# One-token attention plus a gated MLP on one core: w_out cut into five rows a lane and 24 lanes of ten, batches spaced by eight in the output's weights, two output stores of eight lanes

## The chip, the core and the metric

The kernel runs on 1 core of a Trainium2 chip. The metric is the device time of one execution in microseconds; a version's time is the median of its runs. Five engines work side by side, each on its own list in order: TensorE (PE, with its weight loads shown as PEld), VectorE (DVE), ScalarE (ACT), GpSimd (POOL) and SyncE (SP), which here only issues DMAs. Sixteen DMA engines move data between HBM and the on-chip memory of 128 partitions ("lanes").

## The reference

Two branches of a decode step share one normalised input, and their sum is added to the input (all bfloat16):

```python
x  = A_x                                    # (4, 1, 640)
xn = layernorm(x)
# A: attention, 32 heads of 128, one query a batch, cache of 4096 keys
q = (xn @ wq).reshape(4, 1, 32, 128)
p = softmax(q . k_cache * 128 ** -0.5)      # k_cache, v_cache: (4, 32, 4096, 128)
A = (p . v_cache).reshape(4, 1, 4096) @ wo  # wo: (4096, 640)
# B: gated MLP, Fh = 864
z = gelu(xn @ w_in)                         # w_in: (640, 1728)
g = w_sp * layernorm(z[..., 864:]) + b_sp   # one position: scalars
B = (z[..., :864] * g) @ w_out              # w_out: (864, 640)
out = x + A + B
```

The two caches are 134 MB each; wq is 5.2 MB, wo 5.2 MB, w_in 2.2 MB and w_out 1.1 MB.

## The kernel before

**Tiles and buffers.** The caches are read once, in 16 tiles each (8 heads of one batch: 8.39 MB, 65,536 bytes a lane). K tiles use two buffers (`kp`), which also hold wq at the start and the last V tile at the end. V tiles use a single buffer (`vp`), which holds the weights of branch B at the start (`w_sb`: w_in, then w_out) and wo at the end. So the first V tile can be loaded only when branch B is done with `w_sb`, and the third K tile only when the first has been used up. In the text K0, K1, ... and V0, V1, ... are these tiles.

**Start.** x is normalised and turned (`xnT_r`), wq gives the queries (`q_ps`, `qT`). All loads but three small ones go out on SP's queue, in the order in which SP's instructions stand. For this part the order is the scheduler's own: an instruction that must wait for something stands where the scheduler finds it due, and whatever follows on SP waits too.

**Branch B** (`gmlp`): 70 matmuls give z, turned, in `zT` (features on lanes); DVE and ACT apply gelu, layer norm and the gate; the result is `yT`, 128 features on lanes for each of `NFF` = 6 columns and a rest of 96. w_out's first 768 rows lie six to a lane, matching `yT`; the remaining 96 rows lie on `TL` = 16 lanes, `TK` = 6 rows each, loaded with four small DMAs of `TE` = 4 lanes. `ye_ps`/`yE` bring the rest of `yT` onto those 16 lanes with six small matmuls.

**Output.** `out_ps` is one accumulator for x, B and A: the 640 columns are cut into `NQ` = 4 parts of 160, and part q stands on lanes 32q to 32q+3, one lane a batch. `add_out` issues the four matmuls, each with a weight of four columns (the batches). At the end ACT copies `out_ps` to `res`, and four stores of four lanes each write it.

**The loop** has its order written out by hand (`tc.manual_schedule` for PE, DVE, ACT and SP). Before it stand `stage_q(0)`, `gmlp()` and V0's load. For each K tile i: `product` multiplies half the tile by the query on DVE (8.7 us), `fold` adds its halves, `sums` adds up eight-element groups on PE into `s_ps`, `row_sums` finishes the scores. One tile later follow the maximum, `exps`, `own_heads` and `weighted` (p . V on PE); after it the next V load is issued, and after `sums(i, 1)` the next K load. `group_rows`, `group_turn` and `group_proj` normalise eight heads' results, turn them (`oT`) and multiply by wo into `out_ps`. The lines that matter:

```python
stage_q(0)
gmlp()
load_v(0, v_slot("v_nat"))
for i in range(NT):
    product(i, 0)
    ...
    sums(i, 1)
    if i + 2 < NT:
        load_k(i + 2)
```

Of the kernel before, what the change touches and what calls it, by code (L numbers as in the profile page):

```python
# [10 lines left out]
BF16 = mybir.dt.bfloat16  # L11
# [6 lines left out]
def kernel(  # L18
# [45 lines left out]
    WJ = WH * Dh // P  # L64
    WW = 2
    WR = NG * ROWS
    NFF = Fh // P
    TL = 16
    TK = (Fh - NFF * P) // TL
    TE = 4  # L70
    NFC = NFF + TK
    F0 = NFF * P
    TF = TL * TK
    NZ = NFF + 1
    assert F0 + TF == Fh and TF <= P
    NQ = 4
    NO = D // NQ
    REP = GW // Bsz
# [18 lines left out]
    def v_slot(name):  # L97
# [8 lines left out]
    w_sb = v_slot("w_sb")  # L106
    w_in_sb = w_sb[:, 0 : DC * F].rearrange("p (c n) -> p c n", c=DC)
    w_out_sb = w_sb[:, DC * F : DC * F + NFC * D].rearrange("p (k n) -> p k n", k=NFC)
    nc.sync.dma_start(
        out=w_out_sb[:, 0:NFF, :], in_=B_w_out[0 : NFF * P].rearrange("(p k) n -> p k n", k=NFF)  # L110
    )
# [10 lines left out]
    for l in range(TL // TE):  # L122
        nc.sync.dma_start(
            out=w_out_sb[:TL, NFF:NFC, :].rearrange("(e l) k n -> e l (k n)", e=TE)[:, l],
            in_=B_w_out[F0:Fh].rearrange("(e l k) n -> e l (k n)", e=TE, k=TK)[:, l],
        )

    def kv_view(cache, i):
# [23 lines left out]
    WO_CUTS = ((0, WJ), (0, 11, 15, WJ))  # L152

    def load_wo():
        t = v_slot("wo")[:, 0 : HP * WJ * D].rearrange("p (g j n) -> p g j n", g=HP, n=D)
        wo_t.append(t)
        for g in range(HP):
            for j0, j1 in zip(WO_CUTS[g], WO_CUTS[g][1:]):
                nc.sync.dma_start(out=t[:, g, j0:j1, :], in_=wo_v[g][:, j0:j1, :])  # L159
# [3 lines left out]

    ident = const.tile([P, P], BF16)
    make_identity(nc, ident[:])
    ident_f = const.tile([P, P], FP32)
    nc.gpsimd.tensor_copy(out=ident_f[:], in_=ident[:])
    eps_tile = const.tile([P, 1], FP32)
# [52 lines left out]
                stop=stop,  # L221
            )

    add_out(ident[:Bsz, :GW], x_bf, start=True)


    own = const.tile([P, HT], FP32)
# [81 lines left out]
    def gmlp():  # L309
        zz, gw, gt, gz, sq = (gm[n] for n in ("zz", "gw", "gt", "gz", "sq"))  # L310
        zT = ps_pv.tile([P, 2, NZ, Bsz], FP32, tag="pv", name="zT")
        for t in range(2):
            f1 = t * Fh + F0
            w_t = w_in_sb[:, :, t * Fh : f1].rearrange("p c (f k) -> p c k f", k=NFF)
            for k in range(NZ):
                for c in range(DC):
                    nc.tensor.matmul(
                        out=zT[: P if k < NFF else TF, t, k, :],
                        lhsT=w_t[:, c, k, :] if k < NFF else w_in_sb[:, c, f1 : f1 + TF],
                        rhs=xnT[:, c, :],  # L320
                        start=(c == 0),
                        stop=(c == DC - 1),
                    )
        nc.vector.tensor_copy(out=zz[:, :, 0:NFF, :], in_=zT[:, :, 0:NFF, :])
        nc.vector.tensor_copy(out=zz[:TF, :, NFF:NZ, :], in_=zT[:TF, :, NFF:NZ, :])
        nc.vector.tensor_tensor(out=gw, in0=zz, in1=zz, op=ALU.mult)
        nc.vector.tensor_scalar(
            out=gw, in0=gw, scalar1=0.044715, scalar2=1.0, op0=ALU.mult, op1=ALU.add
# [72 lines left out]
            in1=ac_sb[:, None, Bsz : 2 * Bsz].to_broadcast([P, NZ, Bsz]),  # L401
            op=ALU.add,
        )
        yT = work.tile([P, NZ, Bsz], BF16, name="yT")
        nc.vector.tensor_tensor(out=yT[:], in0=gz[:, 0, :, :], in1=sq, op=ALU.mult)
        ye_ps = ps_m.tile([TL, TK, Bsz], FP32, tag="m", name="ye_ps")
        for k in range(TK):
            nc.tensor.matmul(
                out=ye_ps[:, k, :],
                lhsT=ident[:TF, :TF].rearrange("p (f k) -> p k f", k=TK)[:, k, :],  # L410
                rhs=yT[:TF, NFF, :],
                start=True,
                stop=True,
            )
        yE = work.tile([TL, TK, Bsz], BF16, name="yE")
        nc.scalar.copy(out=yE[:], in_=ye_ps[:])
        for k in range(NFC):
            if k < NFF:
                add_out(yT[:, k], w_out_sb[:, k, :])
            else:  # L420
                add_out(yE[:, k - NFF], w_out_sb[:TL, k, :])


    qbcs, scores, sums_ps, maxes, pms, pvs, es = {}, {}, {}, {}, {}, {}, {}
# [213 lines left out]
    def group_turn(g):  # L638
        parts = oTs[g]
        JW = WJ // WW  # L640
        t_ps = ps_m.tile([P, WJ, Bsz], FP32, tag="m", name="t_ps")
        for j in range(WJ):
            nc.tensor.matmul(
                out=t_ps[:, j, :],
                lhsT=parts[j // JW][:, j % JW, :, :],
                rhs=row_batch[:],
                start=True,
                stop=True,
            )
        oTs[g] = const.tile([P, WJ, Bsz], BF16, name=f"oT{g}")  # L650
        nc.scalar.copy(out=oTs[g][:], in_=t_ps[:])

    def group_proj(hg):
        for j in range(WJ):
            add_out(
                oTs[hg][:, j, :],
                wo_t[0][:, hg, j, :],
                stop=(hg == HP - 1 and j == WJ - 1),
            )
# [14 lines left out]
    with tc.manual_schedule(engines={E.PE, E.DVE, E.Activation, E.SP}):  # L674
# [5 lines that stand above are left out]
            at(i - 1, row_sums, 1)  # L680
            at(i - 1, lane_max)
            at(i - 1, turn_max)
            at(i - 1, head_max)
            at(i - 1, spread_max)
            fold(i, 0)
            joined(i - 2, group_rows)
            sums(i, 0)
            joined(i - 2, group_turn)
            at(i - 1, bias)
            at(i - 1, exps)  # L690
            at(i + 1, stage_q)
            at(i - 1, own_heads)
            at(i - 1, weighted)
            if i == 0:
                pass
            elif i < NT - 1:
                load_v(i, v_slot("v_nat"))
            else:
                load_wo()
            at(i - 1, take)  # L700
            product(i, 1)
            row_sums(i, 0)
            fold(i, 1)
            at(i - 1, diag)
            group(i - 1, group_den)
# [3 lines that stand above are left out]
            elif i + 2 == NT:  # L709
                load_v(NT - 1, k_slot("v_last"))  # L710
        L = NT - 1
        row_sums(L, 1)
        lane_max(L)
        joined(L - 1, group_rows)
        turn_max(L)
        head_max(L)
        spread_max(L)
        bias(L)
        exps(L)
        own_heads(L)  # L720
        for c0, c1 in zip(V_CUTS, V_CUTS[1:]):
            weighted(L, c0, c1)
        take(L)
        group_den(HG - 1)
        diag(L)
        group_rows(HP - 1)
        group_proj(0)
        group_turn(HP - 1)
        group_proj(HP - 1)

        res = small.tile([P, NO], BF16, tag="s_sb", name="res", bufs=1)
        nc.scalar.copy(out=res[:], in_=out_ps[:])
        out_v = out.flatten_outer_dims()
        for q in range(NQ):
            queue = nc.scalar if q % 2 else nc.sync
            queue.dma_start(
                out=out_v[:, q * NO : (q + 1) * NO], in_=res[GW * q : GW * q + Bsz]
            )


# [28 lines left out]
```

## Time and profile before

| what | value |
|---|---|
| median of 3 runs | 662.51 us (662.46 to 662.76) |
| profiled execution: span | 661.1 us (661.07 in the trace) |
| median less that span | 1.44 us |
| DVE busy | 491.6 us (74%) |
| PE busy | 295.4 us (45%) |
| ACT / POOL busy | 34.4 us / 2.1 us |
| moved by DMA | 282.55 MB, 427 GB/s over the span |
| mean granted PE clock | 0.712 |

The page gives no time of its own for the profiled execution beside its span, so the span stands for it, and what lies around it is the 1.44 us to the median. The span runs from the first to the last instruction. "busy" leaves out waiting and the issue of DMAs. A row of the timeline has start and duration in us, engine (PEq, SPq: the sequencer of PE, SP), source line, operation, output<-input, count, and in brackets the idle time before it with what ended it.

### The profile page before, as it was taken

The numbers are of one execution on the slowest core, as the hardware profiler recorded it, in microseconds if no ns is written. First come the engines' busy times: TensorE is split into PE (matmuls) and PEld (weight loads), VectorE is DVE, ScalarE is ACT, GpSimd is POOL, SyncE is SP. The second block draws the span as 40 slices with busy tenths as digits, with TensorE's granted clock in tenths as the row PEclk, the third lists the DMA queues.
The fourth block names the chain that finished last, engine by engine and source line by source line (L and its number), as shares of the span: only waits on it lengthen the run. The fifth ranks groups of instructions, "written<-read, shape, count | busy, mean of one in ns | idle before, by whom it ended". The sixth has DMA issues, their size and how long they took to land.

```text
span 661.1 us, 4720 instructions
## 1 busy us (share of the span) xinstructions
PE 295.4 (45%) x2099; PEld 127.9 (19%) x2099; DVE 491.6 (74%) x222; ACT 34.4 (5%) x94; POOL 2.1 (0%) x15
## 2 busy tenths in 40 slices
PE   0513464536426253552625344362634507263656
PEld 0301121212112021220202112120211202031223
DVE  1249999959597795959779569986959699695851
ACT  0300000000000000000000000000000000000000
POOL 1000000000000000000000000000000000000000
PEclk9756676876858687675868757787775768777688
DMA  8999999999999999999999999999999999999996
GB/s 377 456 428 444 428 417 441 429 436 441 436 420 433 432 429 445 440 421 432 424 436 441 440 425 432 420 441 436 437 428 437 425 432 429 440 432 437 432 406 275
DMA packets 5712, 282.55 MB, mean 427 GB/s; under 512 B 680, under 2 KB 812, under 8 KB 1084
## 3 DMA queue, kind: packets, MB, share of 16 engines
q1 hardware_dynamic: 5664, 282.24, 98.9%
q8 instruction: 16, 0.26, 0.2%
q14 instruction: 4, 0.03, 0.0%
q10 hardware_dynamic: 28, 0.01, 0.0%
HBM read 282.24 MB, written 0.01 MB: 427 GB/s over the span
## 4 chain that ended last, share of the span: by engine, by line
DMA 51%; DVE 37%; PE 9%; issue 2%; ACT 1%; SPq 0%; DVEq 0%; ACTq 0%
DMA k_nat<-in_A_k_cache_dram 47%; DVE k_nat L449 22%; DVE k_nat L463 11%; PE s_ps L475 8%; DMA wo<-in_A_wo_dram 4%; DVE s_sb L486 3%; DMA w_sb<-in_B_w_out_dram 1%; ACT p L542 1%; PE pv L568 1%; DVE m L495 1%; PE mT L500 0%; DVE nm L505 0%; DVE pm L553 0%; SPq L159 0%; PE out_ps L216 0%
## 5 line engine op out<-in xcount | busy, mean ns | idle before, releaser
L449 DVE TENSOR_TENSOR k_nat<-k_nat,qbc 128x16384 bf16<-128x16384 bf16 x32 | 278.0, 8688 | 97.8 <-DMA k_nat<-in_A_k_cache_dram 97.8
L475 PE MATMUL s_ps<-k_nat,ident 128*128 128x512 bf16 x528 | 184.8, 528 | 139.3 <-DVE k_nat L463 139.3
L463 DVE TENSOR_TENSOR k_nat<-k_nat 128x8192 bf16<-128x8192 bf16 x31 | 136.7, 4410 | 0.0
L475 PEld LDWEIGHTS <-ident 128*128 128x128 bf16 x528 | 65.3, 129 | 248.3 <-DVE k_nat L463 123.3
L500 PE MATMUL mT<-ident_f,m 128*1 128x128 f32 x16 | 5.9, 366 | 160.0 <-DVE m L495 160.0
L568 PE MATMUL pv<-v_nat,pm 128*32 128x512 bf16 x960 | 56.1, 387 | 0.8 <-DVE pm L553 0.8
L486 DVE TENSOR_REDUCE s_sb<-s_ps 128x128 f32<-128x1024 f32 x32 | 39.0, 1218 | 5.4 <-PE s_ps L475 5.4
L500 PEld LDWEIGHTS mT<-ident_f,m 128*1 128x1 f32 x16 | 1.3, 79 | 167.8 <-DVE m L495 156.2
L568 PEld LDWEIGHTS <-pm 128*32 128x32 bf16 x1024 | 27.1, 100 | 34.3 <-issue 8.5
L553 DVE TENSOR_TENSOR pm<-p,own_c 128x2048 bf16<-128x2048 bf16 x16 | 19.6, 1225 | 15.3 <-ACT p L542 15.3
L542 ACT ACTIVATE p<-s_sb,nb 128x256 bf16<-128x256 f32 x16 | 8.1, 508 | 394.1 <-DVE nb_h L524 394.1
L591 PE MATMUL o_ps<-e,pick 128*32 128x128 f32 x128 | 17.0, 276 | 11.2 <-ACT e L578 11.2
L591 PEld LDWEIGHTS o_ps<-e,pick 128*32 128x32 f32 x128 | 12.7, 109 | 18.7 <-ACT e L578 18.7
L578 ACT COPY e<-pv 128x512 f32<-128x512 f32 x16 | 9.4, 586 | 68.1 <-PE pv L568 60.6
L287 DVE COPY qT<-qT_ps 128x64 bf16<-128x64 bf16 x2 | 0.4, 224 | 15.5 <-PE qT_ps L282 15.5
L516 PE MATMUL nb_ps<-nm,ones_row 1*128 1x8 f32 x32 | 9.2, 359 | 6.0 <-DVE nm L505 6.0
L505 DVE TENSOR_REDUCE nm<-mT 1x8 f32<-1x128 f32 x16 | 4.5, 279 | 7.5 <-PE mT L500 7.5
L516 PEld LDWEIGHTS nb_ps<-nm,ones_row 1*128 1x128 f32 x32 | 7.7, 298 | 10.6 <-DVE nm L505 9.9
L271 PE MATMUL q_ps<-wq,xnT_r 128*32 128x512 bf16 x40 | 4.3, 609 | 11.2 <-DMA wq<-in_A_wq_dram 11.2
L443 ACT CAST qbc<-qbc_ps 128x128 bf16<-128x128 f32 x16 | 4.3, 266 | 92.3 <-PE qbc_ps L435 92.3
L608 PE MATMUL den<-ones_col,acc_h 128*32 128x1 f32 x8 | 1.0, 194 | 16.6 <-DVE acc_h L601 16.6
L495 DVE TENSOR_REDUCE m<-s_sb 128x1 f32<-128x256 f32 x16 | 6.7, 420 | 0.5
(92 smaller groups left out, 70.7 us busy)
## 6 DMA issues: line engine op xcount, KB each, us to landing
wq<-in_A_wq_dram SPq DMA_DIRECT2D x1, 5120.0 KB, 16.3
wo<-in_A_wo_dram SPq DMA_DIRECT2D x1, 2560.0 KB
w_sb<-in_B_w_in_dram SPq DMA_DIRECT2D x1, 2160.0 KB, 20.9
wo<-in_A_wo_dram SPq DMA_DIRECT2D x1, 1760.0 KB
w_sb<-in_B_w_out_dram SPq DMA_DIRECT2D x1, 960.0 KB
wo<-in_A_wo_dram SPq DMA_DIRECT2D x1, 640.0 KB, 25.5
k_nat<-in_A_k_cache_dram SPq DMA_DIRECT2D x16, 39.6
v_nat<-in_A_v_cache_dram SPq DMA_DIRECT2D x15, 33.7
```

Source lines behind the costliest of these rows:

```text
L449: nc.vector.tensor_tensor(out=part(i, u), in0=part(i, u), in1=qbcs[i][:, None, :].to_broadcast([P, UC, Dh]), op=ALU.mult,)
L463: nc.vector.tensor_tensor(out=t[:, :, 0:HD2], in0=t[:, :, 0:HD2], in1=t[:, :, HD2:Dh], op=ALU.add)
L475: nc.tensor.matmul(out=sums_ps[i][:, c : c + SC], lhsT=ident[:], rhs=t[:, c : c + SC, g * RW : (g + 1) * RW], start=(g == 0), stop=(g == n ...
L486: nc.vector.tensor_reduce(out=scores[i][:, u * UC : (u + 1) * UC], in_=sums_ps[i][:], axis=AX.X, op=ALU.add,)
L495: nc.vector.tensor_reduce(out=m1[:], in_=scores[i][:], axis=AX.X, op=ALU.max)
L500: nc.tensor.transpose(out=mT[:], in_=maxes[i][:], identity=ident_f[:])
L516: nc.tensor.matmul(out=nb_ps[:], lhsT=ones_row[:], rhs=maxes[i][:], start=True, stop=True)
L542: nc.scalar.activation(out=probs[i][:], in_=scores.pop(i)[:], func=ACT.Exp, bias=maxes.pop(i)[:], scale=scale_qk, accum_out=accs[hg][:, b ...
L553: nc.vector.tensor_tensor(out=pm[:], in0=probs.pop(i)[:] .rearrange("p (n c) -> p n c", c=CB)[:, :, None, :] .to_broadcast([P, NB, HT, CB] ...
L568: nc.tensor.matmul(out=pvs[i][j * GW : (j + 1) * GW, :], lhsT=pm[:, n, :, :].rearrange("p h c -> p (h c)"), rhs=v_nat[:, n * CB : (n + 1) ...
L578: nc.scalar.copy(out=es[i][:], in_=pvs.pop(i)[:].rearrange("p (c d) -> p c d", d=Dh))
L591: nc.tensor.matmul(out=o_ps[hg // NG][own_rows(hg), :], lhsT=pick[:, c, GW - HT - HT * b : 2 * GW - HT - HT * b], rhs=e[:, c, :], start=(b ...
```

## The change

- **w_out.** `NFF` is 5: five rows to a lane for the first 640 rows. The remaining 224 rows lie on 24 lanes of ten (`TL` = 24, `TK` = 10); that is 240 rows, so the last 16 rows of the main part are loaded a second time, and their weight in `yE` is made zero by the selection matrix `sel`. There are again four small DMAs, now of `TE` = 6 lanes (12,800 bytes a lane instead of 7,680).
- **yE.** 20 selection matmuls instead of 6, with `sel` (an identity between blocks of zeros, kept in `w_sb`).
- **Spaced batches.** The output's weights are 32 columns wide, with each batch in every eighth column and zeros between: `yT` and `yE` are written into a zeroed region of `w_sb`, wo's `oT` into a zeroed region behind wo in V's buffer. So batch b of part q lands on lane 32q + 8b. `add_out` for branch B is called 15 times instead of 12. The new `group_rep` copies the first group's `oT` into that region.
- **Stores.** Two of eight lanes (each two parts by four batches), one on ACT's queue and one on SP's, instead of four of four lanes.

The order of SP's instructions in the built program changes with it: K0's load stands ahead of the four small loads of w_out, which stood ahead of K0 before.

```diff
@@ -64,15 +64,18 @@
     WJ = WH * Dh // P
     WW = 2
     WR = NG * ROWS
-    NFF = Fh // P
-    TL = 16
-    TK = (Fh - NFF * P) // TL
-    TE = 4
+    NFF = 5
+    TL = 24
+    TK = 10
+    TE = 6
     NFC = NFF + TK
     F0 = NFF * P
-    TF = TL * TK
-    NZ = NFF + 1
-    assert F0 + TF == Fh and TF <= P
+    NZ = -(-Fh // P)
+    TF = Fh - (NZ - 1) * P
+    OV = TL * TK - (Fh - F0)
+    IL = P + OV
+    IW = (NZ - NFF - 1) * P + TL * TK
+    assert NZ == NFF + 2 and 0 <= OV < P and IW >= IL + P
     NQ = 4
     NO = D // NQ
     REP = GW // Bsz
@@ -106,6 +109,11 @@
     w_sb = v_slot("w_sb")
     w_in_sb = w_sb[:, 0 : DC * F].rearrange("p (c n) -> p c n", c=DC)
     w_out_sb = w_sb[:, DC * F : DC * F + NFC * D].rearrange("p (k n) -> p k n", k=NFC)
+    y_at = DC * F + NFC * D
+    y_rep = w_sb[:, y_at : y_at + (NZ + TK) * GW].rearrange(
+        "p (k b r) -> p k b r", b=Bsz, r=REP
+    )
+    yT, yE = y_rep[:, 0:NZ], y_rep[:TL, NZ : NZ + TK]
     nc.sync.dma_start(
         out=w_out_sb[:, 0:NFF, :], in_=B_w_out[0 : NFF * P].rearrange("(p k) n -> p k n", k=NFF)
     )
@@ -122,7 +130,7 @@
     for l in range(TL // TE):
         nc.sync.dma_start(
             out=w_out_sb[:TL, NFF:NFC, :].rearrange("(e l) k n -> e l (k n)", e=TE)[:, l],
-            in_=B_w_out[F0:Fh].rearrange("(e l k) n -> e l (k n)", e=TE, k=TK)[:, l],
+            in_=B_w_out[Fh - TL * TK : Fh].rearrange("(e l k) n -> e l (k n)", e=TE, k=TK)[:, l],
         )
 
     def kv_view(cache, i):
@@ -152,8 +160,12 @@
     WO_CUTS = ((0, WJ), (0, 11, 15, WJ))
 
     def load_wo():
-        t = v_slot("wo")[:, 0 : HP * WJ * D].rearrange("p (g j n) -> p g j n", g=HP, n=D)
+        w = v_slot("wo")
+        t = w[:, 0 : HP * WJ * D].rearrange("p (g j n) -> p g j n", g=HP, n=D)
         wo_t.append(t)
+        o_rep = w[:, HP * WJ * D : HP * WJ * (D + GW)]
+        nc.gpsimd.memset(o_rep, 0.0)
+        wo_t.append(o_rep.rearrange("p (g j b r) -> p g j b r", g=HP, b=Bsz, r=REP))
         for g in range(HP):
             for j0, j1 in zip(WO_CUTS[g], WO_CUTS[g][1:]):
                 nc.sync.dma_start(out=t[:, g, j0:j1, :], in_=wo_v[g][:, j0:j1, :])
@@ -163,6 +175,10 @@
 
     ident = const.tile([P, P], BF16)
     make_identity(nc, ident[:])
+    sel = w_sb[:, SLOT - IW : SLOT]
+    nc.gpsimd.memset(sel[:, 0:IL], 0.0)
+    nc.gpsimd.tensor_copy(out=sel[:, IL : IL + P], in_=ident[:])
+    nc.gpsimd.memset(sel[:, IL + P : IW], 0.0)
     ident_f = const.tile([P, P], FP32)
     nc.gpsimd.tensor_copy(out=ident_f[:], in_=ident[:])
     eps_tile = const.tile([P, 1], FP32)
@@ -221,7 +237,12 @@
                 stop=stop,
             )
 
-    add_out(ident[:Bsz, :GW], x_bf, start=True)
+    x_rep = const.tile([Bsz, Bsz, REP], BF16)
+    nc.gpsimd.tensor_copy(
+        out=x_rep[:], in_=ident[:Bsz, :Bsz, None].to_broadcast([Bsz, Bsz, REP])
+    )
+    nc.gpsimd.memset(w_sb[:, y_at : y_at + (NZ + TK) * GW], 0.0)
+    add_out(x_rep[:].rearrange("c b r -> c (b r)"), x_bf, start=True)
 
 
     own = const.tile([P, HT], FP32)
@@ -313,16 +334,20 @@
             f1 = t * Fh + F0
             w_t = w_in_sb[:, :, t * Fh : f1].rearrange("p c (f k) -> p c k f", k=NFF)
             for k in range(NZ):
+                a = (k - NFF) * P
+                n = TF if k == NZ - 1 else P
                 for c in range(DC):
                     nc.tensor.matmul(
-                        out=zT[: P if k < NFF else TF, t, k, :],
-                        lhsT=w_t[:, c, k, :] if k < NFF else w_in_sb[:, c, f1 : f1 + TF],
+                        out=zT[:n, t, k, :],
+                        lhsT=w_t[:, c, k, :]
+                        if k < NFF
+                        else w_in_sb[:, c, f1 + a : f1 + a + n],
                         rhs=xnT[:, c, :],
                         start=(c == 0),
                         stop=(c == DC - 1),
                     )
-        nc.vector.tensor_copy(out=zz[:, :, 0:NFF, :], in_=zT[:, :, 0:NFF, :])
-        nc.vector.tensor_copy(out=zz[:TF, :, NFF:NZ, :], in_=zT[:TF, :, NFF:NZ, :])
+        nc.vector.tensor_copy(out=zz[:, :, 0 : NZ - 1, :], in_=zT[:, :, 0 : NZ - 1, :])
+        nc.vector.tensor_copy(out=zz[:TF, :, NZ - 1, :], in_=zT[:TF, :, NZ - 1, :])
         nc.vector.tensor_tensor(out=gw, in0=zz, in1=zz, op=ALU.mult)
         nc.vector.tensor_scalar(
             out=gw, in0=gw, scalar1=0.044715, scalar2=1.0, op0=ALU.mult, op1=ALU.add
@@ -401,24 +426,27 @@
             in1=ac_sb[:, None, Bsz : 2 * Bsz].to_broadcast([P, NZ, Bsz]),
             op=ALU.add,
         )
-        yT = work.tile([P, NZ, Bsz], BF16, name="yT")
-        nc.vector.tensor_tensor(out=yT[:], in0=gz[:, 0, :, :], in1=sq, op=ALU.mult)
+        nc.vector.tensor_tensor(
+            out=yT[:, :, :, 0], in0=gz[:, 0, :, :], in1=sq, op=ALU.mult
+        )
         ye_ps = ps_m.tile([TL, TK, Bsz], FP32, tag="m", name="ye_ps")
         for k in range(TK):
-            nc.tensor.matmul(
-                out=ye_ps[:, k, :],
-                lhsT=ident[:TF, :TF].rearrange("p (f k) -> p k f", k=TK)[:, k, :],
-                rhs=yT[:TF, NFF, :],
-                start=True,
-                stop=True,
-            )
-        yE = work.tile([TL, TK, Bsz], BF16, name="yE")
-        nc.scalar.copy(out=yE[:], in_=ye_ps[:])
+            for w in range(2):
+                n = (P, TF)[w]
+                a = P * (1 - w) + k
+                nc.tensor.matmul(
+                    out=ye_ps[:, k, :],
+                    lhsT=sel[:n, a : a + TK * (TL - 1) + 1 : TK],
+                    rhs=yT[:n, NFF + w, :, 0],
+                    start=(w == 0),
+                    stop=(w == 1),
+                )
+        nc.scalar.copy(out=yE[:, :, :, 0], in_=ye_ps[:])
         for k in range(NFC):
             if k < NFF:
-                add_out(yT[:, k], w_out_sb[:, k, :])
+                add_out(yT[:, k].rearrange("p b r -> p (b r)"), w_out_sb[:, k, :])
             else:
-                add_out(yE[:, k - NFF], w_out_sb[:TL, k, :])
+                add_out(yE[:, k - NFF].rearrange("p b r -> p (b r)"), w_out_sb[:TL, k, :])
 
 
     qbcs, scores, sums_ps, maxes, pms, pvs, es = {}, {}, {}, {}, {}, {}, {}
@@ -647,13 +675,19 @@
                 start=True,
                 stop=True,
             )
-        oTs[g] = const.tile([P, WJ, Bsz], BF16, name=f"oT{g}")
-        nc.scalar.copy(out=oTs[g][:], in_=t_ps[:])
+        if g == HP - 1:
+            nc.scalar.copy(out=wo_t[1][:, g, :, :, 0], in_=t_ps[:])
+        else:
+            oTs[g] = const.tile([P, WJ, Bsz], BF16, name=f"oT{g}")
+            nc.scalar.copy(out=oTs[g][:], in_=t_ps[:])
+
+    def group_rep(g):
+        nc.scalar.copy(out=wo_t[1][:, g, :, :, 0], in_=oTs[g][:])
 
     def group_proj(hg):
         for j in range(WJ):
             add_out(
-                oTs[hg][:, j, :],
+                wo_t[1][:, hg, j].rearrange("p b r -> p (b r)"),
                 wo_t[0][:, hg, j, :],
                 stop=(hg == HP - 1 and j == WJ - 1),
             )
@@ -709,6 +743,8 @@
             elif i + 2 == NT:
                 load_v(NT - 1, k_slot("v_last"))
         L = NT - 1
+        for g in range(HP - 1):
+            group_rep(g)
         row_sums(L, 1)
         lane_max(L)
         joined(L - 1, group_rows)
@@ -730,11 +766,12 @@
 
         res = small.tile([P, NO], BF16, tag="s_sb", name="res", bufs=1)
         nc.scalar.copy(out=res[:], in_=out_ps[:])
-        out_v = out.flatten_outer_dims()
-        for q in range(NQ):
-            queue = nc.scalar if q % 2 else nc.sync
+        out_v = out.flatten_outer_dims().rearrange("b (q n) -> q b n", n=NO)
+        QH = NQ // 2
+        for h, queue in enumerate((nc.scalar, nc.sync)):
             queue.dma_start(
-                out=out_v[:, q * NO : (q + 1) * NO], in_=res[GW * q : GW * q + Bsz]
+                out=out_v[QH * h : QH * (h + 1)],
+                in_=res[GW * QH * h : GW * QH * (h + 1) : REP],
             )
 
 
```

## The prediction

> **What bounds the kernel now.** I read the page first: slices, DMA rows, chain. DMA stands at 9 in nearly every slice, so the end is set by the stream of loads.
>
> ```profile
> DMA  8999999999999999999999999999999999999996
> q1 hardware_dynamic: 5664, 282.24, 98.9%
> DMA 51%; DVE 37%; PE 9%; issue 2%; ACT 1%; SPq 0%; DVEq 0%; ACTq 0%
> ```
>
> 282.24 MB in 661.1 us is 427 GB/s (26.7 a DMA engine), and a K or V tile of 8.39 MB takes 19.4-19.6 us of the stream. Any stretch in which the queue runs dry is lost for good; any other wait costs nothing. So the question is when SP issues each load. The timeline of SP (start, duration, what):
>
> ```profile
> 1.65 0.47 SPq L121 DMA_DIRECT2D w_sb<-in_B_w_in_dram  x1
> 2.16 3.76 SPq L123 DMA_DIRECT2D w_sb<-in_B_w_out_dram  x4
> 5.96 16.17 SPq L139 DMA_DIRECT2D k_nat<-in_A_k_cache_dram  x2
> 35.70 0.33 SPq L145 DMA_DIRECT2D v_nat<-in_A_v_cache_dram  x1
> 76.89 0.33 SPq L139 DMA_DIRECT2D k_nat<-in_A_k_cache_dram  x1
> 95.04 0.33 SPq L145 DMA_DIRECT2D v_nat<-in_A_v_cache_dram  x1
> 107.95 0.33 SPq L139 DMA_DIRECT2D k_nat<-in_A_k_cache_dram  x1
> ```
>
> The third K load (K2) goes out at 76.89. By bytes V0, the last load queued ahead of it, ends at 43.2 (K0 landed) + 2 x 19.4 = 82; in the trace's packet records the engines finish V0 at 79.8-81.5. An issue brings its first packet about 1.0 us later (the first, 0.73, had packets from 1.76). So K2 came with 2 to 3 us to spare: the thinnest lead of the run. Next, the timeline of PE and DVE up to there:
>
> ```profile
> 23.82 3.67 PEld L317 LDWEIGHTS <-w_sb 128*128 128x128 bf16 x70 [0.98 <-DMA w_sb<-in_B_w_out_dram]
> 33.38 0.19 DVE L405 TENSOR_TENSOR yT<-gm_t 128x28 bf16<-128x28 f32 x1
> 43.24 8.69 DVE L449 TENSOR_TENSOR k_nat<-k_nat,qbc 128x16384 bf16<-128x16384 bf16 x1 [9.67 <-DMA k_nat<-in_A_k_cache_dram]
> 70.52 6.34 PE L475 MATMUL s_ps<-k_nat,ident 128*128 128x512 bf16 x16 [7.48 <-DVE k_nat L463]
> ```
>
> gmlp starts when the four small w_out loads land, not w_in: issued by 5.92, they landed near 23.8, after wq and w_in, so the queue serves in order. gmlp runs 23.82-33.57 = 9.75 us to yT, inside DVE's 9.67 us of idle before K0's product. From 43.24 DVE has work without a gap until sums(0,1) ends at 76.86 and releases K2.
>
> **The change, part by part.** *Order of SP.* In the built program of the changed kernel SP issues w_out's main part, wq, w_in, then K0, and the four small loads only after it: the first small one waits for w_in to land, and that wait holds the three others, K1 and V0 behind it. PE's first zT weight load still waits for all four, as before. This is the step that decides.
>
> w_in landed at 1.65 + 20.9 = 22.55. The main w_out load loses 1280 B on 128 lanes = 164 KB, 0.38 us: w_in lands at 22.2. K0, already queued, takes 19.4: 41.6 (by packet records, 8 x 2.418 us an engine, 40.8-41.1). Then the small loads: before, 123 KB in four-lane transfers took 23.8 - 22.55 = 1.2 us, about 100 GB/s, four engines' worth. Now it is 307 KB on six lanes each: at 100 GB/s 3.0 us, at the full 427 GB/s 0.7. I take 1.5 times the four-lane rate, 2.0 us, since six lanes stand in place of four: they land at 43.0-43.6, say 43.3. The Trainium skill ("DMA: Bandwidth & Descriptors", "Why a DMA increments its semaphore by 16 and not by 1") has a DMA run on the largest k up to 16 that divides its outer dimension: six engines here, an estimate of 1.9 us by 26.7 GB/s each. The trace's quarter rate for four lanes agrees with it.
>
> *gmlp.* zT from 43.3 instead of 23.82: +19.5. The chain to yT is the same DVE, ACT and PE steps (70 zT pairs in both; yT only moves into w_sb): 9.75 us, end 53.05. DVE runs in order, so product(0,0) waits for yT instead of K0: 43.24 becomes 53.0, +9.8. V0's issue moves by +19.5 and by 14 more ye and 12 more out_ps matmuls at 20-30 ns, to about 55.9; K1 holds the queue to 60.5 or later: no loss. SP's issue of K1 moves from 22.1 to about 24.6 (four issues of 0.58), under K0: no loss.
>
> *K2.* 76.89 + 9.8 = 86.7, with first packets at 87.7. PE's 16 sums before it ran 6.34 at a low clock (0.56 in this stretch); others in the chain took 5.0-6.0, so 85.3 to 86.7; I take 86.4, packets at 87.4. The engines were through with V0 at 79.8-81.5 before; now ten have 10 KB less (-0.38), four 10 KB and two 41 KB more (+0.4, +1.5): most are dry from 79.5-80 on. Lost: 87.4 - 80.0 = 7.4 us for the engines that ended last before. Some of those had lost 0.7 us at 80-81 us in single slow packets, which a common restart need not repeat: 6.7-7.4, taken 7.1.
>
> *After it.* V1's issue moves to 104.8, packets 105.8; K2 holds the queue until 87.4 + 19.4 = 106.8. K3's to 117.8 against V1's end at 126. From there DVE (29 us of work a tile) catches up with the stream (38.9 a tile) and every later load is on time: one stall, not sixteen.
>
> *The end.* Before, the last wo piece let PE go at 657.27:
>
> ```profile
> 657.27 0.67 PE out_ps L216 x20
> 658.01 0.29 ACT res L732
> ```
> ```profile
> 658.33 0.64 SPq L736 DMA_DIRECT2D out_dram<-res  x2
> 658.34 0.62 ACTq L736 DMA_DIRECT2D out_dram<-res  x2
> ```
>
> One store a queue instead of two takes away the second issue, 0.3 us; the packet records put the second stores 0.35 after the first: -0.35 us. A store of eight lanes instead of four: 20 ns a row, nothing. The weights of out_ps are 32 columns wide instead of 4. 4-column pairs came every 20-24 ns (64 in 1.4 us), 128-column ones (L317) every 52 ns; 32 columns are nearer to the first: 27, so the last 20 cost +0.1 us, with 0 and +0.6 as ends. The Trainium skill ("TensorE: Matmul & The Clock Gate", "LDWEIGHTS (loading the stationary operand)") gives columns / 1.2 in ns: 27 for 32 columns by its formula, 107 for 128, where this trace shows half of that; by it the sum is the same.
>
> *Covered.* GpSimd's memsets and copies at the start (15 instructions took 2.1 us) and the reordered DVE reductions lie ahead of wq's landing at 17.5; the memset in load_wo and the copy group_rep (ACT, about 0.2) follow pv(14) at 630.9, and ACT is next wanted at 643: cover 10 us. The overlap of the new remainder, 20 KB, is in the lanes above.
>
> Sum: +7.1 - 0.35 + 0.1 = +6.85. Span 661.07 + 6.85 = 667.9. The median lies 1.44 above the profiled span, taken as unchanged: 669.4 us, 1.0% slower.
>
> **Rivals.** *No stall (not slower).* If the small loads came through beside K0 rather than behind it, gmlp would stay in DVE's idle 9.67 us. It decides at zT: a start up to 33.5 costs nothing, and up to about 36 K2's lead still covers it. What is left is the store's -0.35 and up to 0.4 either way from the moved bytes, since the engines end wo between 653.3 and 657.1 and the last are among those that carry the 16 instruction packets of q8: 661.7-662.3. Against it: the old small loads, issued by 5.92, sat behind wq and w_in until 23.8. Chance 0.05. The Trainium skill (first page named, "Queues, rings and completion order") has each engine take descriptors in ring order, which speaks against it too.
>
> *A second stall.* V1's lead over K2's end is 1.0 us. PE's sums(1,0) and pv(0) stand before its issue; at a clock of 0.5 instead of 0.73 they take 1-3 us longer, and the stream is dry again: up to +2, 671.4. For it: clocks of 0.5 to 1.0 in the slices. Against: the lead is still positive. Chance 0.15.
>
> *A slow tail.* At the 128-column price the 44 matmuls from 655.7 (same place before the end) take 2.3 us, past wo's landing by 0.75, and the last 20 0.4 more: +1.1, 670.4. Against: t_ps and zT load four times the columns. Chance 0.06.
>
> **How the numbers follow.** My forecast has 0.72, the others 0.05, 0.15, 0.06, and 0.02 is left. The forecast's own bounds: small loads 0.7 to 3.0 us (-1.3, +1.0), sums at 5.0 us (-1.1), slow packets repeated (+0.3): 667.2 to 670.7. The second stall lengthens it to 671.4; the no-stall case is left out. A measurement of this kernel tells 0.2% (1.3 us) from no change. Faster 0.01, same 0.05 (no stall), slower 0.94.
>
> **What would show it.** Right: zT starts near 43.3, DVE's first product near 53, K2's issue near 86, one slice with low GB/s at 80-87 us (the fifth or sixth), later slices as before, one store a queue. Wrong: zT before 36; or GB/s without a hole; or a second hole near 107 us; or over 4.0 us between the last wo landing and the end of the span.

## The result, and the profile after

The changed kernel takes 669.38 us (median of 4 runs, 669.26 to 669.93) against 662.63 us for the kernel before beside it: ratio 1.0103, 95% interval 1.0092 to 1.0115. It is 1.0% slower. The profiled execution has a span of 667.4 us (667.38 in the trace) and took 669.26 us.

Page of the changed kernel: the DMA row of the 40 slices, the data queue, and the shares of the chain.

```profile
DMA  8999799999999999999999999999999999999996
q1 hardware_dynamic: 5674, 282.26, 98.0%
DMA 48%; DVE 39%; PE 9%; issue 3%; ACT 1%; SPq 0%; DVEq 0%; ACTq 0%
```

Almost the same bytes (282.26 MB, 282.24 before) take 98.0% of a span that is 6.3 us longer, and one slice, the fifth (66.7 to 83.4 us), has dropped to 7. Timeline of SP, changed kernel:

```profile
1.64 0.50 SPq L129 DMA_DIRECT2D w_sb<-in_B_w_in_dram  x1
2.19 0.67 SPq L147 DMA_DIRECT2D k_nat<-in_A_k_cache_dram  x1
22.60 3.00 SPq L131 DMA_DIRECT2D w_sb<-in_B_w_out_dram  x4
25.73 0.35 SPq L147 DMA_DIRECT2D k_nat<-in_A_k_cache_dram  x1
56.14 0.34 SPq L153 DMA_DIRECT2D v_nat<-in_A_v_cache_dram  x1
85.34 0.33 SPq L147 DMA_DIRECT2D k_nat<-in_A_k_cache_dram  x1
105.08 0.33 SPq L153 DMA_DIRECT2D v_nat<-in_A_v_cache_dram  x1
```

K0 stands ahead of the four small loads, the first of which waits for w_in (22.27 by the packet records) and goes out at 22.60. K2 goes out at 85.34 instead of 76.89. Timeline of PE and DVE:

```profile
43.50 3.15 PE L340 MATMUL zT<-xnT_r,w_sb 128*128 128x4 bf16 x70 [20.32 <-DMA w_sb<-in_B_w_out_dram]
52.46 0.28 DVE L429 TENSOR_TENSOR w_sb<-gm_t 128x28 bf16<-128x28 f32 x1
52.57 8.69 DVE L477 TENSOR_TENSOR k_nat<-k_nat,qbc 128x16384 bf16<-128x16384 bf16 x1
79.84 5.47 PE L503 MATMUL s_ps<-k_nat,ident 128*128 128x512 bf16 x16 [8.35 <-DVE k_nat L491]
```

zT waits for the small loads until 43.50. K0 landed by 41.6, but DVE, which takes its work in order, is in gmlp's chain (its last step is the L429 row) and starts the first product only behind it, at 52.57; before, the 9.67 us ahead of that product were a wait for K0. Four stretches of 4 us (the last two numbers are the DMA engines' busy share and GB/s; a packet counts where it starts):

```profile
76.00:80.00 4.00, 0.15 (x1) 0.13 (x2) 4.00 (x2) 0.00 (x0) 0.00 (x0) 0.60 0.91 393
80.00:84.00 4.00, 4.00 (x11) 1.40 (x10) 4.00 (x1) 0.00 (x0) 0.00 (x0) 0.55 0.00 0
84.00:88.00 4.00, 1.31 (x7) 0.39 (x4) 4.00 (x1) 0.00 (x0) 0.00 (x0) 1.00 0.75 262
88.00:92.00 4.00, 0.83 (x3) 0.57 (x3) 3.60 (x5) 0.00 (x0) 0.00 (x0) 0.80 1.06 459
```

In the kernel before, the second stretch was full:

```profile
80.00:84.00 4.00, 0.93 (x3) 0.57 (x3) 3.41 (x4) 0.00 (x0) 0.00 (x0) 0.50 1.04 442
```

In the changed kernel no data packet starts between 80 and 84 us. By the packet records the engines finish V0 between 79.65 and 81.60, and the first packet of K2 starts at 86.29: for 4.7 us no byte moves at all. From the trace's packet records I add up, between 24 and 600 us, the time in which an engine had no packet, and divide by the 16 engines: 6.04 us in the changed kernel, 0.17 before. wo's last packet ends at 663.27 instead of 657.13, +6.14. Then the tail:

```profile
662.24 0.44 ACT L679 CAST wo<-t_ps 128x64 bf16<-128x64 f32 x1 [3.70 <-PE t_ps L671]
662.73 1.31 PE L232 MATMUL out_ps<-wo 128*32 128x160 bf16 x64 [0.53 <-ACT wo L679]
664.14 0.29 ACT L768 CAST res<-out_ps 128x160 bf16<-128x160 f32 x1 [1.46 <-PE out_ps L232]
664.46 0.61 SPq L772 DMA_DIRECT2D out_dram<-res  x1
664.46 0.64 ACTq L772 DMA_DIRECT2D out_dram<-res  x1
```

From wo's last packet to the end of the span it is 4.11 us, 3.94 before. PE no longer waits for wo but for the copy of oT, which takes 0.44 us into spaced columns and took 0.21. That moves nothing here: the copy to `res` starts 0.87 us after wo's last packet, 0.88 before. The 0.17 us lie behind it, with the stores (3.24 us, 3.06 before).

### The profile page after: what moved, and what is told of

Read it like the earlier page. It is cut to its first block, busy times and chain, and to the rows that moved or that the text cites. A ratio compares the mean times of both kernels' runs of the same rounds, so it can differ in the third digit from the quotient of the medians.

```text
span 667.4 us, 4789 instructions
## 1 busy us (share of the span) xinstructions
PE 300.7 (45%) x2125; PEld 130.2 (20%) x2125; DVE 491.5 (74%) x222; ACT 35.2 (5%) x95; POOL 4.2 (1%) x21
## 3 DMA queue, kind: packets, MB, share of 16 engines
q1 hardware_dynamic: 5674, 282.26, 98.0%
HBM read 282.26 MB, written 0.01 MB: 423 GB/s over the span
## 4 chain that ended last, share of the span: by engine, by line
DMA 48%; DVE 39%; PE 9%; issue 3%; ACT 1%; SPq 0%; DVEq 0%; ACTq 0%
DMA k_nat<-in_A_k_cache_dram 36%; DVE k_nat L477 23%; DVE k_nat L491 11%; PE s_ps L503 6%; DMA v_last<-in_A_v_cache_dram 6%; DMA w_sb<-in_B_w_in_dram 3%; DMA w_sb<-in_B_w_out_dram 3%; DVE s_sb L514 3%; PE pv L596 1%; ACT p L570 1%; DVE m L523 1%; PE zT L340 0%; PE mT L528 0%; DVE nm L533 0%; SPq L131 0%
## 5 line engine op out<-in xcount | busy, mean ns | idle before, releaser
L503 PE MATMUL s_ps<-k_nat,ident 128*128 128x512 bf16 x528 | 188.2, 536 | 126.5 <-DVE k_nat L491 126.5
L340 PE MATMUL zT<-xnT_r,w_sb 128*128 128x4 bf16 (+1 forms) x70 | 3.1, 183 | 20.3 <-DMA w_sb<-in_B_w_out_dram 20.3
## 6 DMA issues: line engine op xcount, KB each, us to landing
wo<-in_A_wo_dram SPq DMA_DIRECT2D x1, 640.0 KB, 24.6
```

Source lines behind the costliest of these rows:

```text
L503: nc.tensor.matmul(out=sums_ps[i][:, c : c + SC], lhsT=ident[:], rhs=t[:, c : c + SC, g * RW : (g + 1) * RW], start=(g == 0), stop=(g == n ...
```

## Experiments

Theory: the place of K0 on SP delays zT, gmlp, DVE's first product and so K2, and K2's delay beyond its lead is lost once. Rivals: the layout of w_out, the spaced batches or the stores cost the time; or the loss has no threshold.

### The order on SP alone

```diff
-    for l in range(TL // TE):
-        nc.sync.dma_start(
-            out=w_out_sb[:TL, NFF:NFC, :].rearrange("(e l) k n -> e l (k n)", e=TE)[:, l],
-            in_=B_w_out[F0:Fh].rearrange("(e l k) n -> e l (k n)", e=TE, k=TK)[:, l],
-        )
...
     load_k(0)
+    for l in range(TL // TE):
+        nc.sync.dma_start(
... (the same load)
```

> The kernel before with one thing of the change alone: on SP, K0's load stands ahead of the four small w_out loads. The layout of w_out (16 lanes of six rows), the weights of four columns and the four stores are the old ones. Theory (the place of the small loads is the whole loss): zT starts near 43 us, the first product on DVE near 52.5, K2 goes out at 85.3 to 86.5, the stream is empty for about 6 us and the span is 667 to 668: ratio to the kernel before 1.009 to 1.0105, as with the whole change. Rival (the 24 lanes, the spaced batches or the new stores cost the time): 1.000 within 0.2%, with K2 out near 77.

Measured: 670.85 us, ratio 1.0126 (1.0112 to 1.0139). SP:

```profile
2.16 0.75 SPq L134 DMA_DIRECT2D k_nat<-in_A_k_cache_dram  x1
2.95 3.66 SPq L158 DMA_DIRECT2D w_sb<-in_B_w_out_dram  x4
86.80 0.33 SPq L134 DMA_DIRECT2D k_nat<-in_A_k_cache_dram  x1
```

zT starts at 43.39, the product at 53.04; the engines are empty for 7.50 us. The small loads are issued at once here, and zT is as late as in the changed kernel: it is their place behind K0 in the queue that delays them, not SP's wait for w_in. The order alone reproduces the whole loss and comes out above it, and above the range I gave, so the rest of the change doesn't cost and may gain. Part of the difference is K2, 1.46 us later: zT took 3.73 instead of 3.15, and PE's 16 sums 6.46 instead of 5.47. Another part turns up in the last experiment.

### How much lead K2 has

Before the first product DVE reduces 16, 28 or 40 of K0's chunks (128 elements a lane each) into a column that nobody reads.

```diff
         load_v(0, v_slot("v_nat"))
+        nc.vector.tensor_reduce(
+            out=spare[:], in_=part(0, 0)[:, 0:40, :], axis=AX.XY, op=ALU.max
+        )
```

> The kernel before with nothing but a delay: ahead of the first product DVE reduces 40 of K0's chunks into a scratch column, about 6 us of work whose result is not used. Theory (K2's issue has 2 to 3 us to spare, and all beyond is lost once and for good): K2 goes out near 83, its packets start near 84 against engines that are through with V0 at 79.8 to 81.5, so 2.5 to 4 us are lost: ratio 1.004 to 1.006, one slice with low GB/s behind V0 and none later. Rival without a threshold: the whole 6 us, 1.009. Rival in which the stream makes up for it: 1.000.

> The kernel before with the delay of the earlier run cut to 16 of K0's chunks: 40 of them took DVE 5.49 us, so 2.2 us here. With 40, K2 went out at 82.37 and the engines were without a packet for 3.2 us on average behind V0. Theory (a lead of 1.6 to 2.3 us, a loss only beyond it): K2 goes out at 79.1, its packets start at 80.1, the engines are empty for 0.2 to 0.7 us on average, ratio 1.000 to 1.0015. Rival without a threshold: all of the 2.2 us, 1.0033.

> The same delay with 28 of K0's chunks: 3.85 us. Theory (a lead of 1.6 to 2.3 us, beyond it microsecond for microsecond): K2 goes out at 80.7, the engines are empty for 1.4 to 2.0 us on average, ratio 1.002 to 1.0038, between the delays of 16 and 40 chunks. Rival without a threshold: 1.0058.

The longest delay on DVE, and K2's issue after it:

```profile
43.33 5.49 DVE L679 TENSOR_REDUCE spare<-k_nat 128x1 f32<-128x5120 bf16 x1 [9.89 <-DMA k_nat<-in_A_k_cache_dram]
82.37 0.33 SPq L139 DMA_DIRECT2D k_nat<-in_A_k_cache_dram  x1
```

| kernel | delay, us | K2 issued | engines empty, us | ratio (95%) |
|---|---|---|---|---|
| before | 0 | 76.89 | 0.17 | 1 |
| 16 chunks | 2.29 | 79.17 | 0.30 | 1.0028 (1.0019 to 1.0038) |
| 28 chunks | 3.89 | 80.37 | 1.26 | 1.0041 (1.0027 to 1.0055) |
| 40 chunks | 5.49 | 82.37 | 3.18 | 1.0060 (1.0045 to 1.0075) |
| changed kernel | | 85.34 | 6.04 | 1.0103 (1.0092 to 1.0115) |
| order alone | | 86.80 | 7.50 | 1.0126 (1.0112 to 1.0139) |

From the third row on, the empty time is K2's issue less 79.2 (1.2, 3.2, 6.1, 7.6): microsecond for microsecond beyond a lead of 79.2 - 76.9 = 2.3 us. So the threshold is there for empty time, but the times came out above my theory (1.0060 at its upper end, 1.0041 and 1.0028 beyond it). By its time alone, the run with 16 chunks fits the rival without a threshold (1.0033); the runs with 28 and 40 chunks don't (1.0058 and 1.009 were forecast by it), and the packet records, with 0.30 us empty after a delay of 2.29, decide for the threshold. What the theory lacked shows in the packet records: when a load arrives just as the engines run dry, each engine's first packet is slow. Over the usual 2.418 us, K2's first packets cost on average over the engines 0.53, 0.62, 0.61, 0.58 and 0.70 us in the five lower rows, and 0.11 before. It is paid even where hardly anything is empty (16 chunks). With 16 chunks the profiled run took 663.92 us, the median 664.71; what the other executions lost beyond it is not in a trace and stays open. That a restart makes these packets slow is read from where they stand, not tested by itself.

### The first product ahead of gmlp

The changed kernel with SP's new order, but DVE doesn't wait for branch B.

```diff
         stage_q(0)
+        product(0, 0)
         gmlp()
         load_v(0, v_slot("v_nat"))
         for i in range(NT):
-            product(i, 0)
+            if i > 0:
+                product(i, 0)
```

> The changed kernel with the first product of K0 put ahead of gmlp in the hand-written order, so that DVE doesn't wait for branch B with K0 landed. SP's order stays the changed one (K0 ahead of the small loads). Theory (the loss is DVE's first product waiting for gmlp, and so K2's issue, not the place of the loads in the queue as such): the product starts near 41.5 us, gmlp's DVE steps follow it from 50.1 and end near 56, K2 goes out at 79.5 to 81 instead of 85.34, and the stream is dry for 0 to 1.5 us instead of 6: ratio 1.000 to 1.003. Rival (the small loads behind K0 hold up the stream itself): 1.008 or more.

Measured: 665.21 us, ratio 1.0038 (1.0024 to 1.0051), between theory and rival. The first product starts at 41.65 and K2 goes out at 80.27, as the theory has it:

```profile
59.63 0.33 SPq L153 DMA_DIRECT2D v_nat<-in_A_v_cache_dram  x1
80.27 0.33 SPq L147 DMA_DIRECT2D k_nat<-in_A_k_cache_dram  x1
100.02 0.33 SPq L153 DMA_DIRECT2D v_nat<-in_A_v_cache_dram  x1
```

The engines are empty for 0.94 us instead of 6.04. So DVE's wait is the path of the loss. What I missed: gmlp, now later, holds V0 until 59.63, and three loads in a row arrive just in time; their first packets cost 0.56, 0.50 and 0.34 us.

### The old order with the new layout

Small loads to neighbouring lanes; SP then issues them ahead of K0.

```diff
-            out=w_out_sb[:TL, NFF:NFC, :].rearrange("(e l) k n -> e l (k n)", e=TE)[:, l],
-            in_=B_w_out[Fh - TL * TK : Fh].rearrange("(e l k) n -> e l (k n)", e=TE, k=TK)[:, l],
+            out=w_out_sb[TE * l : TE * (l + 1), NFF:NFC, :].rearrange("e k n -> e (k n)"),
+            in_=B_w_out[Fh - TL * TK : Fh].rearrange("(l e k) n -> l e (k n)", e=TE, k=TK)[l],
```

> The changed kernel with one thing undone: each small w_out load goes to six neighbouring lanes instead of every fourth lane, and SP then issues the four ahead of K0, as before the change. The 24 lanes of ten rows, the spaced batches and the two stores stay. Theory: zT starts near 25 us, gmlp is back inside DVE's wait for K0, K2 goes out near 77, and the hole of 6 us in the stream is gone; what is left is the tail of the changed kernel (+0.2 us in the span) and up to 0.5 us outside of it: ratio 0.999 to 1.0015. Rival (the layout, the spaced weights or the stores cost the time, wherever the loads stand): 1.008 to 1.0105.

Measured: 666.44 us, ratio 1.0053 (1.0041 to 1.0066): neither. The hole is gone (0.20 us empty), but K0 lands late, and DVE waits for it:

```profile
48.55 8.69 DVE L477 TENSOR_TENSOR k_nat<-k_nat,qbc 128x16384 bf16<-128x16384 bf16 x1 [16.65 <-DMA k_nat<-in_A_k_cache_dram]
81.47 0.33 SPq L147 DMA_DIRECT2D k_nat<-in_A_k_cache_dram  x1
```

The small loads' packets of 12,800 bytes take 1.22 us (median, up to 1.60), and 0.479 each in the changed kernel, where they go to every fourth lane; K0's packets beside them take up to 5.34 us instead of 2.42. My edit had put in a new cost. Two runs test that; the first is the same edit in the kernel before, where TE is 4:

```diff
-            out=w_out_sb[:TL, NFF:NFC, :].rearrange("(e l) k n -> e l (k n)", e=TE)[:, l],
+            out=w_out_sb[TE * l : TE * (l + 1), NFF:NFC, :].rearrange("e k n -> e (k n)"),
```

> The kernel before with one thing changed: each of the four small w_out loads goes to four neighbouring lanes instead of every fourth lane; bytes, number of loads and the order of SP are the old ones. With six neighbouring lanes the packets took 1.22 us (median) instead of 0.479, 2.5 times as long. Theory (loads to neighbouring lanes get in each other's way): packets of 7,680 bytes take 0.7 to 0.9 us instead of 0.291, K0's first packets beside them are slow too, K0 lands 1.5 to 4 us later, and the time goes up by 1 to 3.5 us: ratio 1.0015 to 1.005. Rival (the six engines or the 307 KB were the cost, not which lanes): 1.000 within 0.1%, packets of 0.29 us.

Measured: 663.59 us, ratio 1.0013 (1.0004 to 1.0022). Packets of 7,680 bytes take 0.42 us in the median and up to 0.98 instead of 0.291; the first product starts at 44.55 instead of 43.24. The small loads and the start of K0 do get slower; with four lanes the price is below the range I gave. But the neighbours alone don't make it: of the first load's four packets, one on each engine and on neighbouring lanes, three run side by side from 21.84 us, and all four take 0.291. The slow ones begin at 22.14, beside K0's packets. (In the run with six lanes, too, the first four, from 21.68 to 21.75, take 0.479.) The edit also makes each load's source one contiguous piece of w_out, and no run separates that from the lanes. The Trainium skill ("SBUF — State Buffer", "Door 1: The DMA port swizzle (why `[64,N]` ≈ `[32,N]`)") has four neighbouring lanes share one DMA port. By that, four engines writing to four neighbours would take four times as long, an estimate of 1.16 us; the median here is 1.45 times, the slowest packet 3.4 times and the first ones not slower at all, so the trace doesn't show the port to be the cause.

In the changed kernel, the same 24 lanes with every small load spread again but cut by rows, all issued ahead of K0:

```diff
-    for l in range(TL // TE):
+    for k0, k1, te in ((0, 7, 6), (7, 10, 24)):
+        for l in range(TL // te):
...
-            out=w_out_sb[:TL, NFF:NFC, :].rearrange("(e l) k n -> e l (k n)", e=TE)[:, l],
+            out=w_out_sb[:TL, NFF + k0 : NFF + k1, :].rearrange("(e l) k n -> e l (k n)", e=te)[:, l],
```

> The changed kernel with the same rest of w_out on the same 24 lanes, every small load again on every fourth lane, but cut by rows: four loads of six lanes with the first seven rows and one of 24 lanes with the last three. SP then issues all five ahead of K0. The spaced batches and the two stores stay. Theory (the order on SP was the loss of the change, and neighbouring lanes were the loss of the run before this one): zT starts near 24.5 us, the first product near 43.5, K2 goes out near 77, no hole, packets of the small loads take 0.34 us each as their bytes ask (0.48 us for 12,800), ratio 0.9985 to 1.001. Rival (24 lanes of ten rows ahead of K0 cost the time wherever the lanes lie): 1.004 to 1.006, as with neighbouring lanes, with K0 landing near 48.

Measured: 663.34 us, ratio 1.0011 (1.0002 to 1.0020), just above the theory's range; K2 out at 77.84, 0.11 us empty. With the order put back and the lanes spread, 0.9 of the 1.03% are gone: the new layout needs no hole. A second cut, 12 in place of 24 for the last three rows, asked where the rest comes from:

> The run with the small loads cut by rows (four of six lanes with seven rows, ahead of K0), with the last three rows in two loads of every second lane instead of one load of 24 neighbouring lanes; SP then issues K0 when wq has landed, near 17.4 us, still ahead of w_in's end at 22. Theory (the 0.7 us that were left came from the load of neighbouring lanes): packets of 8,960 bytes take 0.34 us throughout instead of up to 0.69, K0's first packets 2.42 us instead of up to 3.09, the first product starts near 43.4 instead of 43.96, ratio 0.999 to 1.0005. Rival (307 KB on six engines cost it, wherever they lie): 1.001 again.

Measured: 663.28 us, ratio 1.0013 (1.0004 to 1.0022), the first product at 44.01: no better, the theory falls. (In the first, the packets of the load to 24 neighbouring lanes had taken 0.149 to 0.153 us, none of them slow.) In both, packets of 8,960 bytes took up to 0.69 and 0.73 us, and K0's packets were slow by 0.44 and 0.46 us an engine in the first 30 us (0.00 before). Why they disturb each other is open: four spread engines don't in the kernel before, and in the changed kernel six don't either, where all 24 packets of 12,800 bytes take 0.479 us beside K1's first ones of 2.42.

### Spaced batches and stores alone

The kernel before with the output's 32-column weights and the two stores; then with four stores of four spaced lanes. The second differs from the first in the stores alone (the loop around them is left out):

```diff
             queue.dma_start(
-                out=out_v[QH * h : QH * (h + 1)],
-                in_=res[GW * QH * h : GW * QH * (h + 1) : REP],
+                out=out_v[:, q * NO : (q + 1) * NO],
+                in_=res[GW * q : GW * (q + 1) : REP],
             )
```

> The kernel before with the spaced batches (output weights of 32 columns) and the two stores of eight lanes, but the old w_out (six rows a lane, 16 lanes of six) and the old order on SP. First theory (the prediction's working: one store a queue saves a second issue): 0.3 us shorter than the kernel with four stores of this call, ratio to the kernel before 0.9995. Second theory (what the trace of the changed kernel shows: a store of two parts by four batches takes 0.61 to 0.64 us to issue, as long as two old ones, and its first packet comes 1.24 to 1.59 us after the start of the issue instead of 0.76): 0.3 us longer than with four stores, ratio 1.0005. Both are within what the timing can tell, so the rows of the stores and of the last packets decide: first packets 0.75 us after the issue for the first theory, 1.2 us or more for the second. In neither is there a hole behind V0.

> The kernel before with the spaced batches alone: output weights of 32 columns, and four stores of four lanes as before (each from every eighth lane). Old w_out and old order on SP. It prices the 32 columns by themselves: if they cost what four columns do (20.5 ns a matmul in the changed kernel's trace), the ratio is 1.000 within 0.1% and the stores are issued in 0.3 us each with first packets 0.76 us after; if they cost as much as 128 columns (52 ns), the last 20 matmuls take 1.04 us instead of 0.67 and the time goes up by 0.4 us or more, up to 1.1.

Measured: 661.86 us, ratio 0.9992 (0.9983 to 1.0001), with two stores; 662.43 us, 0.9997 (0.9989 to 1.0006), with four. The times tell neither from the kernel before. The tail with four spaced stores:

```profile
655.68 0.64 PE L225 MATMUL out_ps<-wo 128*32 128x160 bf16 x20 [0.58 <-DMA wo<-in_A_wo_dram]
656.75 1.30 SPq L758 DMA_DIRECT2D out_dram<-res  x2
656.75 1.52 ACTq L758 DMA_DIRECT2D out_dram<-res  x2
```

The last 20 matmuls take 0.64 us with 32 columns, and 0.64 with 4 in the timeline of before: the width is free. Two four-lane stores take 1.30 and 1.52 us to issue from every eighth lane, and took 0.64 and 0.62 from neighbouring lanes. From the copy to `res` to the end of the span it is 3.06 us before, 4.04 with four spaced stores, 3.23 with two, 3.24 in the changed kernel. So two stores save 0.8 us of what spacing costs, and 0.2 is left. My second theory had the first packets right (1.24 us after the issue) and the comparison wrong: four spaced stores are dearer than two, not cheaper.

### Where the buffers start

Both last kernels were no slower than before in spite of a longer tail: wo's last packet ends at 655.6 and 655.7, 1.5 us earlier than before, with K2 out at 76.80 and 77.18. Their 65,536-byte packets are shorter. The next run is the kernel before with its K and V buffers 64 bytes further down in each lane:

```diff
+    pad = const.tile([P, 32], BF16, name="pad")
+    nc.gpsimd.memset(pad[:, 0:1], 0.0)
...
-        oTs[g] = const.tile([P, WJ, Bsz], BF16, name=f"oT{g}")
+        pool = work if g == HP - 1 else const
+        oTs[g] = pool.tile([P, WJ, Bsz], BF16, name=f"oT{g}")
```

> The kernel before with its K and V buffers 64 bytes further down in each lane, and nothing else: the second group's oT moves to another pool and a pad of 64 bytes stands among the constants (one memset of a column on GpSimd more). In the built programs the buffers start at 20032, 85568 and 151104 bytes before the change (each 64 over a multiple of 512) and at 19968, 85504 and 151040 with the spaced batches (multiples of 512). From the tenth tile on nearly all 65,536-byte packets took 2420 ns or more in the six kernels run so far with the first addresses, and 2418 in the seven with the second; on average over the engines that is 0.7 us in the run. Theory (the start of the buffers makes it): packets of 2418 ns here too, span and time 0.7 us shorter with the old stores and the old w_out, ratio 0.9983 to 0.9993. Rival (something else of the spaced batches makes it, or it is the execution): packets of 2420 ns, ratio 1.000.

Measured: 661.36 us (661.20 to 661.53), ratio 0.9980 (0.9971 to 0.9990): 0.2% faster than the kernel before, a little more than I gave. SP and the tail:

```profile
75.79 0.33 SPq L139 DMA_DIRECT2D k_nat<-in_A_k_cache_dram  x1
655.69 0.64 PE L218 MATMUL out_ps<-wo,oT 128*4 128x160 bf16 x20 [0.60 <-DMA wo<-in_A_wo_dram]
656.75 0.65 SPq L739 DMA_DIRECT2D out_dram<-res  x2
```

The tail is the old one (two stores in 0.65 us), and wo's last 20 matmuls start at 655.69 instead of 657.27. The median packet takes 2418 ns, 2420 before; from the twelfth tile on 99% take 2418 or less, and 6% before (85% took 2420 or more, so "nearly all" in my expectation was too strong). Packets up to 60 ns over 2418 add up to 0.10 us an engine, 0.85 before; longer ones to 0.58 and 0.74. That is 0.9 of the 1.4 us by which wo ends earlier; the rest I have not traced. The Trainium skill ("DMA: Bandwidth & Descriptors", "How a descriptor splits into AXI transactions") has a descriptor that starts off a 256-byte boundary fetch the bytes back to it as well. 64 bytes are two beats of 32 on top of 2,048, an estimate of 2.4 ns for these packets; the trace has 2. The page speaks of what is fetched, though, and here it is the written side that starts off the boundary.

The changed kernel has the good addresses too, by accident: 0.12 us instead of 0.85. That is the gain that hides in it.

## Why the prediction was right

The forecast was 669.4 us and 1.0% slower; measured were 669.38 and 1.03%. The mechanism stands: each step of the chain was found in the trace, and single runs reproduce the loss (the order alone) and take it away (the first product ahead of gmlp; the order put back). The sizes are less good than the total, and one of the four signs of being wrong did appear: from wo's last packet to the end of the span it is 4.11 us, over the 4.0 that was set.

- **Order, small loads, gmlp.** Forecast 43.3 for the landing, 53.0 for the product; zT started at 43.50, the product at 52.57. The chain to yT's end took 9.24 us instead of 9.75, since zT ran 3.15 us instead of 3.73 (both for 70 matmuls).
- **K0's neighbours in the queue.** V0 at 55.9 (56.14), K1 at 24.6 (25.73), both without loss, as forecast.
- **K2.** 86.4 forecast, 85.34 measured: zT, and sums of 5.47 us, which I had taken at 6.0 within 5.0 to 6.3. The lead "2 to 3 us" is 2.3.
- **Lost in the stream: mis-sized term, 7.1 against 6.14.** K2's issue, 1.06 us earlier than forecast, is the main part of the difference. Empty time is 5.9 more than before. Slow packets beyond 60 ns add 0.9, and the new buffer addresses take 0.7 off, a term that the sum did not have. That restarted packets "need not repeat" their slowness was wrong: 15 of 16 did, 0.58 us.
- **A second stall** (rival, 0.15): V1 went out at 105.08, and no empty time of note followed, but 14 of its first packets were slow, 0.43 us. The rival happened, without a hole, at about a fifth of its price.
- **The end: mis-sized term, -0.25 against +0.17.** The store's -0.35 rested on "20 ns a row, nothing": the spaced source lanes cost more in the issue than the second store saved. The 32 columns cost 0, not 0.1, so the rival of a slow tail fell too. The copy of oT, 0.23 us longer, was not in the sum, and cost nothing here.
- **Around the span: 1.44 against 1.88** (669.26 less 667.38). In all twelve experiments' profiled runs it is 1.77 to 1.90. My 1.44 set a span against the median of other executions.

The sum as measured: 661.07 + 6.14 + 0.17 + 1.88 = 669.26. Errors of -1.0, +0.4 and +0.4 cancelled, so the agreement to 0.02 us is luck; the sign and the 1% are not.

## What to carry to other kernels

Where a stream of loads is the bound, look for the load with the thinnest lead, and ask of each edit what it puts ahead of the step that releases that load: up to the lead the engines hardly ran empty here (the run with 2.29 us of delay still lost 0.28%, slow first packets among it), beyond it every microsecond was lost. Look at the order of the DMA queue in the built program, since a changed view of a small load moved an 8 MB load past it. And compare the addresses of the large buffers: moving them by 64 bytes was worth 0.2% here.

## What the hardware did that I had not expected

- Buffers that start 64 bytes past a multiple of 512 take 2420 ns instead of 2418 for most 65,536-byte packets (256 and 512 were not told apart).
- Small loads cut to neighbouring lanes (and with that to contiguous sources) slow the load behind them and are slowed beside it: 12,800-byte packets of 1.22 us instead of 0.479, K0's packets up to 5.34 us. The first small packets, side by side, were not slow; the cause is open.
- After the stream ran dry or nearly so, each engine's first packet took 0.53 to 0.70 us longer on average, even where only 0.30 us an engine were empty.
- A four-lane store from every eighth lane takes 0.65 to 0.76 us to issue, from neighbouring lanes 0.31.
- A matmul with a weight of 32 columns takes as long as with 4: 20 in 0.64 us.
